# Turning the state's attention weights with 32x32 blocks and on-chip transfers, in batches 2 to 7

## The chip, the cores and the metric

The kernel runs on one core of one Trainium2 chip. The metric is the device time of one execution in microseconds (us); lower is better. All data is float32. The core has five engines that work side by side and meet at semaphores: TensorE (PE in the profile, with its weight loads as PEld), VectorE (DVE), ScalarE (ACT), GpSimd (POOL) and SyncE (SP), which here only issues transfers.

## The reference

Two things are computed one after the other. First a small attention between 512 tokens and 32 states, in 8 batches of 8 heads with 64 dimensions. It is read in both directions: the tokens read the states (`xread`), and the states read the tokens (`sread`). Then every row of the joined result goes through a gated feed-forward layer with 2048 hidden columns.

```python
# x: (8, 8, 512, 64), state: (8, 8, 32, 64)
scores = scale * np.matmul(x, state.transpose(0, 1, 3, 2))
a = softmax(scores)
xread = np.matmul(a, state)
scores2 = scale * np.matmul(state, x.transpose(0, 1, 3, 2))
a2 = softmax(scores2)
sread = np.matmul(a2, x)
attn_out = np.concatenate([xread, sread], axis=2)
...
x = attn_out.transpose(0, 2, 1, 3).reshape(8 * 544, 512)
h = x @ w_in          # 512 x 2048
g = h * np.cos(h)
out = g @ w_out       # 2048 x 512
```

(`softmax` stands for the lines that subtract the maximum, take the exponential and divide by the sum.) The change is about one step on the way to `sread`: for `a2 @ x` on TensorE, the weights `a2` must lie with the tokens on the partitions, and they come out of the exponential with the states on the partitions.

## The kernel before, in words

**Tiles and steps.** Rows of tokens are worked on in 8 batches (`b`), and the hidden columns in 16 tiles of 128. So there are 16 steps per batch, numbered 0 to 15 here, and 16 more for the states' own rows at the end. In every step TensorE computes one hidden tile (`hidden`, L462), ScalarE and VectorE turn it into `h * cos(h)` (`gate`, L468; `gate2`, L471; `gate3`, L476 and L477; `gate4`, L483), and TensorE multiplies tiles of three steps earlier with blocks of `w_out` (`product`, L527). The hidden tile lies in one of two PSUM banks, so the hidden matmul of step s needs that `gate4` of step s-2 is done. The second layer uses a recursive block scheme over pairs of batches (an even and an odd one): in odd batches there are extra differences of gated tiles (`minus`, L489), some on VectorE and some on GpSimd, and finished sums are turned and stored (`store`, L554 and L560), four transfers for one turned tile.

**Attention beside it.** The attention of batch b+1 is computed during the steps of batch b, spread over the steps by a plan that is written out by hand: `plan(b)` returns for every step what TensorE (`pe`), ScalarE (`x_act`, `y_act`) and VectorE (`x_dve`, `y_dve`) do besides. Within a step the program order is: hidden matmul, `pe`, `gate`, `gate2`, `x_act`, `x_dve`, `gate3`, one pending store, `gate4`, differences, `y_act`, `y_dve`, then products. Each engine keeps that order. "Batch b" below always means the steps of batch b, in which the attention of batch b+1 is worked on.

**The parts that matter.** Buffers: `xT` (128 partitions, 4 x 512) holds first the transposed tokens of a batch; later its first half is `spread` and then `a2T`, its second half `z2`. `z2` has heads and states on the partitions (32 states for each of 4 values of k, and j = 0 or 1 in the columns) and the 512 tokens in the columns. `a2T` has the 128 tokens of a group c on the partitions.

- `load_tokens` (L284): 16 transfers into `xT`, followed by `load_x` (L112), 4 transfers. Both are issued on SyncE right after `reads` 1 of the batch before, in `part` (L449 to L453). `tokens_turned` (L293) then turns `xT` in 32x32 blocks on VectorE.
- `scores` (L311), `max1`, `spread1` (L331), `shift`, `max2`, `exps` (L352, L357), `sums` (L325, L367), a second `spread1`, and `norm1` (L375), which reads `spread`, the first half of `xT`.
- `turn` (L381): eight 128x128 transposes of `z2` on TensorE into the two PSUM banks `at`; `turn_kept` (L386): two copies of ScalarE from there into `a2T`.
- `reads` (L398): two times 8 matmuls of `a2T` with the tokens `x_b`, into `at`; `keep` (L409) takes the result away on VectorE; `keep2` and `keep3` (L415, L420) turn it into `sT`.
- `products` (L311) multiply state and `w_in` for the first layer, and also use the `at` banks: in batches from 2 on at steps 0, 4, 9 and 14.

Before the change, batches 2 to 6 run the parts `tokens_turned` at steps 1 and 2 (batch 1: at 2 and 3), `scores` at 5, the second `spread1` at 8 in `y_dve`, `norm1` at 9 in `x_dve`, `turn` at 10, `reads` 0 at 11, `reads` 1 and `keep` at 12, and `keep2` at 15. Batch 1 follows the same steps from 5 on. Batch 0 has its own plan, for its own attention's end and that of batch 1.

SyncE works through one queue in program order: stores, `load_tokens`, `load_x`; the loads of the weights are over after the first steps of batch 1, but for two near the end.

Of the kernel before, what the change touches and what calls it, by code (L numbers as in the profile page):

```python
# [23 lines left out]
def kernel(  # L24
# [8 lines left out]
    nc = tc.nc  # L33

    B, H, S, D = x.shape
    Ns = state.shape[2]
    Dm, Dff = moe_w_in.shape
    P = 128
    NK = Dm // P
# [206 lines left out]
    class Attention:  # L246
# [141 lines left out]

        def reads(self, j):
            cols = slice(2 * D * j, 2 * D * j + 2 * D)
            for c in range(NC):
                x_c = self.x_b[:, c].rearrange("p (k j) d -> p j k d", j=2)
                for k in range(0, NK, 2):
                    rows = slice(Ns * k, Ns * k + 2 * Ns)
                    nc.tensor.matmul(  # L398
                        out=at[0][rows, cols], lhsT=self.a2T[:, j, c, rows],
                        rhs=x_c[:, j, k:k + 2], start=(c == 0),  # L400
                        stop=(c == NC - 1), tile_position=(0, Ns * k))
# [324 lines left out]
    def plan(b):  # L726
        pe, x_act, y_act, x_dve, y_dve = [
            {s: [] for s in range(NF)} for _ in range(5)]

        def prod(s, b, nt, *bank):  # L730
            pe[s].append((b, "products", nt) + bank)
            if b == 1 and nt > 0:
                x_dve[s].append((b, "products_taken", nt) + bank)
            else:
                x_act[s].append((b, "products_kept", nt) + bank)

        def pairs(s, b, name, kept, i):
            pe[s] += [(b, name, i), (b, name, i + 1)]
            x_act[s].append((b, kept, i))
            y_act[s].append((b, kept, i + 1))  # L740

        def early(b, s):
            if b == 1:
                pairs(s[0], b, "tokens", "tokens_kept", 0)
                pairs(s[1], b, "tokens", "tokens_kept", 2)
            else:
                for k in range(NK):
                    to = (x_dve, y_dve)[k % 2]
                    to[s[k // 2]].append((b, "tokens_turned", k))
            pe[s[2]].append((b, "scores"))  # L750
            x_dve[s[2]].append((b, "max1"))
            x_dve[s[3]].append((b, "spread1"))
            y_dve[s[3]].append((b, "shift"))
            x_dve[s[4]].append((b, "max2"))
            y_act[s[4]].append((b, "exps"))
            x_dve[s[5]].append((b, "sums"))
            y_dve[s[5]].append((b, "spread1"))
            x_dve[s[6]].append((b, "norm1"))

        def late(b, s):  # L760
            pairs(s[0], b, "turn", "turn_kept", 0)
            pe[s[1]].append((b, "reads", 0))
            pe[s[2]].append((b, "reads", 1))
            x_dve[s[2]].append((b, "keep"))
            if len(s) > 3:
                turned(b, s[3])

        def turned(b, s):
            pe[s].append((b, "keep2"))
            x_act[s].append((b, "keep3"))  # L770


        if b == 0:
            pe[0].append((0, "products", 0, SIDE, HC, WC))
            y_dve[0].append((0, "products_taken", 0, SIDE, HC, WC))
            prod(7, 0, 2, SIDE)
            prod(11, 0, 3)
            prod(13, 1, 0, MAIN)
            late(0, (1, 2, 3, 4))
            early(1, (5, 6, 7, 8, 9, 10, 11))  # L780
            late(1, (12, 13, 14))
        else:
            bank = (SIDE,) if b == 1 else ()
            if b == 1:
                turned(1, 0)
            prod(0, b, 1, *[MAIN for _ in bank])
            prod(4, b, 2, *bank)
            prod(9, b, 3, *bank)
            if b + 1 < B:
                prod(14, b + 1, 0)  # L790
                early(b + 1, (1 + (b == 1), 2 + (b == 1), 5, 6, 7, 8, 9))
                late(b + 1, (10, 11, 12, 15))
        return pe, x_act, y_act, x_dve, y_dve


# [20 lines left out]
    for step, t in enumerate(all_tiles):  # L816
        s = step % NF
        if s == 0 and t.b < B:
            steps = plan(t.b)
# [81 lines left out]
```

## Time and profile before

| | |
|---|---|
| median of 3 runs | 798.88 us (798.44 to 799.73) |
| the profiled execution's own time | 797.16 us |
| its span, first to last instruction | 795.4 us |
| mean granted TensorE clock | 0.992 |
| L381, transposes of `z2` on TensorE | 64, 273 ns each as listed, 8.3 us |
| L386, copies of the turned weights on ScalarE | 16, 573 ns each, 9.2 us |
| L398, `reads` on TensorE | 256, 279 ns each as listed, 17.5 us |
| L293, turning of the tokens on VectorE, 128x512 | 24, 703 ns each |
| L331, `spread1` on VectorE, 128x1024 | 16, 1237 ns each |
| L284, token transfers of 64 KB | 96, median 2.3 us from issue to landing |
| L560, stores of 64 KB | 128, median 2.0 us from issue to landing |

How to read the profile: the page gives each engine's busy time and share of the span, then the chain of work that ended last, followed back from the end to what released each instruction. Groups of instructions are listed by line, with mean duration and the idle time ahead of them. A timeline row gives start, length, engine, line, operation, tiles, shapes and how many instructions of that kind follow one another; a bracket at its end names the idle time before it and what ended it. A matmul of float32 data appears as two instructions, a transpose as one, so one hidden tile is a row of `x4` and the turning of one batch a row of `x8`. Matmuls are pipelined: the length of a row goes beyond the start of the next.

### The profile page before, as it was taken

Reading aid. Unit: us, or ns where it says so; the run is one execution under the profiler, and the core shown is the slowest. Engines: PE = TensorE matmul, PEld = TensorE weight load, DVE = VectorE, ACT = ScalarE, POOL = GpSimd, SP = SyncE. Lnnn points to the kernel's source line nnn. Section 1 sums busy time; section 2 is a strip of 40 time slices with the busy share of each in tenths; the row PEclk is TensorE's granted clock in tenths of the full one; section 3 lists DMA queues with packets and bytes.
Section 4 is the critical chain, followed back from the end, with each engine's and each line's share of the span. In section 5 each row is a group of like instructions: output and inputs, shape, how many; then the busy total and the mean of one; then the engine's idle time right before and its main releaser. Section 6 shows DMA issues by size and latency. Waiting matters only on the chain.

```text
span 795.4 us, 7553 instructions
## 1 busy us (share of the span) xinstructions
PE 767.1 (96%) x2654; PEld 339.8 (43%) x2654; DVE 437.5 (55%) x689; ACT 389.5 (49%) x626; POOL 178.3 (22%) x119
## 2 busy tenths in 40 slices
PE   8879889999999999999999999999999999999996
PEld 4333333343444444444344434444444444455553
DVE  5779886742554466743564467735554446432431
ACT  3877954644455444734463436443563445322222
POOL 3243357775000000451000000650000004610200
PEclk9999999999999999999999999999999999999999
DMA  8485371032010611150002410340100114000021
GB/s 237 159 227 196 110 155 28 0 55 53 0 26 5 116 24 16 30 103 0 14 13 48 85 27 3 54 78 0 27 0 1 27 27 131 1 0 15 13 47 33
DMA packets 161957, 43.49 MB, mean 55 GB/s; under 512 B 153920, under 2 KB 153920, under 8 KB 161920
## 3 DMA queue, kind: packets, MB, share of 16 engines
q1 hardware_dynamic: 161216, 42.75, 24.7%
q8 instruction: 21, 0.34, 0.2%
q10 hardware_dynamic: 576, 0.13, 0.1%
q0 software_dynamic: 128, 0.13, 0.1%
q14 instruction: 16, 0.13, 0.1%
HBM read 34.08 MB, written 8.91 MB: 54 GB/s over the span
## 4 chain that ended last, share of the span: by engine, by line
PE 79%; DVE 10%; ACT 7%; issue 1%; DMA 1%; POOL 0%; SPq 0%; DVEq 0%; POOLq 0%
PE o L527 44%; PE h L462 26%; PE at L311 4%; PE o L644 3%; DVE q L471 2%; PE at L398 2%; DVE g_all L483 1%; ACT q L476 1%; DVE xT L331 1%; ACT q L477 1%; DVE aT L375 1%; ACT q L468 1%; ACT L477 1%; DVE w_in L234 1%; ACT xT L357 1%
## 5 line engine op out<-in xcount | busy, mean ns | idle before, releaser
L462 PE MATMUL h<-aT,sw 128*128 128x512 f32 x512 | 245.8, 603 | 14.9 <-DVE g_all L483 12.3
L527 PE MATMUL o<-g_all,w_out 128*128 128x512 f32 x512 | 236.4, 598 | 1.2 <-POOL w_out L239 1.2
L468 ACT ACTIVATE q<-h 128x512 f32<-128x512 f32 (+1 forms) x144 | 82.2, 571 | 268.2 <-PE h L462 268.2
L489 POOL TENSOR_TENSOR g_all<-g_all 128x512 f32<-128x512 f32 x80 | 112.1, 1421 | 452.4 <-DVE g_all L483 448.8
L471 DVE SCALAR_TENSOR_TENSOR q<-q,h 128x512 f32<-128x512 f32 (+1 forms) x144 | 94.2, 654 | 206.0 <-ACT q L468 205.8
L527 PE MATMUL o<-g_all,s 128*128 128x512 f32 x384 | 177.3, 598 | 0.0
L483 DVE TENSOR_TENSOR g_all<-h,q 128x512 f32<-128x512 f32 (+1 forms) x144 | 94.8, 658 | 122.3 <-ACT q L477 116.3
L462 PEld LDWEIGHTS h<-aT,sw 128*128 128x128 f32 x512 | 97.1, 192 | 141.6 <-issue 110.1
L527 PEld LDWEIGHTS o<-g_all,w_out 128*128 128x128 f32 x512 | 94.0, 190 | 126.6 <-issue 119.0
L476 ACT ACTIVATE q<-q 128x512 f32<-128x512 f32 (+1 forms) x144 | 87.5, 608 | 97.2 <-DVE q L471 97.2
L527 PEld LDWEIGHTS o<-g_all,s 128*128 128x128 f32 x384 | 70.8, 190 | 91.7 <-issue 87.5
L477 ACT ACTIVATE q<-q,halfpi 128x512 f32<-128x512 f32 (+1 forms) x144 | 100.5, 698 | 4.5
L239 POOL TENSOR_TENSOR w_out<-w_out,s 128x1024 int32<-128x1024 int32 x10 | 23.9, 2389 | 82.3 <-DVE w_out L234 79.6
L489 DVE TENSOR_TENSOR g_all<-g_all 128x512 f32<-128x512 f32 x48 | 33.2, 692 | 1.6
L436 ACT COPY sw<-at 128x512 f32<-128x512 f32 x50 | 26.8, 588 | 9.0 <-PE at L311 9.0
L462 PE MATMUL h<-sT,w_in 128*128 128x256 f32 x128 | 30.2, 379 | 0.0
L644 PE MATMUL o<-w_out,g_all 128*128 128x512 f32 x64 | 29.6, 592 | 0.0
L462 PEld LDWEIGHTS h<-sT,w_in 128*128 128x128 f32 x128 | 24.3, 190 | 10.1 <-issue 6.2
L311 PE MATMUL at<-w_in,stT 64*32 64x512 f32 x400 | 27.9, 616 | 0.0
L239 POOL TENSOR_TENSOR w_in<-w_in,s 128x1024 int32<-128x1024 int32 (+1 forms) x10 | 19.4, 1936 | 32.1 <-DVE w_in L234 22.1
L533 DVE SCALAR_TENSOR_TENSOR held<-o,held 128x512 f32<-128x512 f32 x40 | 25.3, 676 | 2.3 <-PE o L527 2.3
L554 DVE STREAM_TRANSPOSE ot<-held 128x512 f32<-128x512 f32 x32 | 22.2, 693 | 0.0
(85 smaller groups left out, 444.5 us busy)
## 6 DMA issues: line engine op xcount, KB each, us to landing
out_dram<-ot SPq DMA_DIRECT2D x136, 64.0 KB, 2.0
g_all<-in_moe_w_out_dram SPq DMA_DIRECT2D x8, 1024.0 KB, 5.0
g_all<-in_moe_w_in_dram SPq DMA_DIRECT2D x6, 1024.0 KB, 5.3
xT<-in_x_dram SPq DMA_DIRECT2D x96, 64.0 KB, 2.3
x_b<-in_x_dram SPq DMA_DIRECT2D x24, 256.0 KB, 4.5
x_b<-in_x_dram SPq DMA_DIRECT2D x16, 128.0 KB, 3.9
g_all<-in_moe_w_in_dram SPq DMA_DIRECT2D x4, 512.0 KB, 6.0
x_b<-in_moe_w_out_dram SPq DMA_DIRECT2D x1, 1024.0 KB, 5.7
```

Source lines behind the costliest of these rows:

```text
L239: nc.gpsimd.tensor_tensor(bits, bits, e.bitcast(I32), op=ALU.add)
L311: nc.tensor.matmul(out=(to or at)[j][Ns * k:Ns * k + Ns, 0:n], lhsT=w[D * j:D * j + D, self.b, Ns * k:Ns * k + Ns], rhs=r(slice(D * j, D * ...
L436: (copy or nc.scalar.copy)(sw_of[self.b, nt][:, j, c0:c1], to[j][:, 0:c1 - c0])
L462: nc.tensor.matmul(out=t.hp, lhsT=t.lhs(i), rhs=t.rhs(i), start=(i == 0), stop=(i == t.kn - 1))
L468: nc.scalar.activation(t.q, t.hp, func=ACTF.Copy, bias=MAGIC)
L471: nc.vector.scalar_tensor_tensor(out=t.q, in0=t.q, scalar=MAGIC, in1=t.hp, op0=ALU.subtract, op1=ALU.subtract)
L476: nc.scalar.activation(t.q, t.q, func=ACTF.Abs)
L477: nc.scalar.activation(t.q, t.q, func=ACTF.Sin, bias=halfpi, scale=-TWO_PI)
L483: nc.vector.tensor_tensor(t.g, t.hp, t.q, op=ALU.mult)
L489: engine.tensor_tensor(out, a, b, op=ALU.subtract)
L527: nc.tensor.matmul(out=acc[bank][ch], lhsT=w[:, i, P * ch:P * ch + P], rhs=g.g, start=(i == 0), stop=(i == NH - 1))
L644: nc.tensor.matmul(out=acc[MAIN][i], lhsT=t.g[:, P * i:P * i + P], rhs=w_out[:, :, t.f, :], start=(n == 0), stop=(n == NF - 1))
```

## The change

For batches 2 to 7 `turn` and `turn_kept` are no longer put into the plan. In their place VectorE turns `z2` within itself in 32x32 blocks (`turn_blocks`), after the second `spread1`, and 16 transfers on SyncE (`turn_moved`) bring the blocks from `z2` to their partitions in `a2T`, after `norm1`. Each transfer takes the 32 partitions of one k and the blocks of one q (a group of 32 partitions of the target), for both j and all four c: 32 partitions with 8 runs of 32 elements on either side, 32 KB. `reads`, `keep` and what hangs on them go one step later, `tokens_turned` from steps 1 and 2 to steps 2 and 3 in batches 2 to 6. `keep2` stays at 15. Batches 0 and 1 are turned as before.

```diff
@@ class Attention
+        def turn_blocks(self):
+            blocks = self.z2.rearrange("p j (t i) -> p (j t) i", i=32)
+            nc.vector.transpose(out=blocks, in_=blocks)
+
+        def turn_moved(self):
+            nq = P // 32
+            src = self.z2.rearrange("p j (c q n) -> p q (j c) n", q=nq, n=32)
+            dst = self.a2T.rearrange("p j c m -> p (j c) m")
+            for k in range(NK):
+                rows = slice(Ns * k, Ns * k + Ns)
+                for q in range(nq):
+                    nc.sync.dma_start(out=dst[32 * q:32 * q + 32, :, rows],
+                                      in_=src[rows, q])
@@ def early(b, s)
             x_dve[s[5]].append((b, "sums"))
             y_dve[s[5]].append((b, "spread1"))
             x_dve[s[6]].append((b, "norm1"))
+            if b > 1:
+                y_dve[s[5]].append((b, "turn_blocks"))
+                x_dve[s[6]].append((b, "turn_moved"))
 
         def late(b, s):
-            pairs(s[0], b, "turn", "turn_kept", 0)
+            if b < 2:
+                pairs(s[0], b, "turn", "turn_kept", 0)
@@ def plan(b)
                 prod(14, b + 1, 0)
-                early(b + 1, (1 + (b == 1), 2 + (b == 1), 5, 6, 7, 8, 9))
-                late(b + 1, (10, 11, 12, 15))
+                early(b + 1, (2, 3, 5, 6, 7, 8, 9))
+                late(b + 1, (11, 12, 13, 15))
```

## The prediction, made before the result was known

> **What bounds the kernel now.** I read the page first (engine shares, the chain of waits by line), then the groups with shapes kept apart, then the timeline of the steps that the change touches, once in an even batch and once in an odd one.
>
> ```profile
> PE 767.1 (96%) x2654; PEld 339.8 (43%) x2654; DVE 437.5 (55%) x689; ACT 389.5 (49%) x626; POOL 178.3 (22%) x119
> ...
> PE 79%; DVE 10%; ACT 7%; issue 1%; DMA 1%; POOL 0%; SPq 0%; DVEq 0%; POOLq 0%
> ```
>
> TensorE holds the end: 79% of the chain. VectorE holds 10%, so there are places where it releases TensorE, and the steps in question must be looked at one by one. First the even batch 4, steps 10 and 11 (rows are start, length, engine and line):
>
> ```profile
> 413.10 0.65 DVE L471 SCALAR_TENSOR_TENSOR q<-q,h 128x512 f32<-128x512 f32 x1
> 413.68 1.21 DVE L375 TENSOR_TENSOR aT<-aT,xT 128x1024 f32<-128x1024 f32 x1
> 413.92 1.88 PE L462 MATMUL h<-aT,sw 128*128 128x512 f32 x4
> 415.64 1.04 PE L381 MATMUL at<-ident,xT 128*128 128x128 f32 x8
> 416.51 3.60 PE L527 MATMUL o<-g_all,w_out 128*128 128x512 f32 x8
> 419.95 1.88 PE L462 MATMUL h<-aT,sw 128*128 128x512 f32 x4
> ```
>
> Starts on TensorE follow one another without a gap. The eight transposes of L381 hold it from 415.64 to 416.51, 0.87 us, though each is listed with 273 ns: they overlap. The same steps in the odd batch 3:
>
> ```profile
> 326.02 3.01 POOL L489 TENSOR_TENSOR g_all<-g_all 128x512 f32<-128x512 f32 x2 [132.10 <-DVE g_all L483]
> ...
> 326.58 1.24 DVE L331 STREAM_TRANSPOSE xT<-m 128x1024 f32<-128x1024 f32 x1
> 327.74 0.65 DVE L471 SCALAR_TENSOR_TENSOR q<-q,h 128x512 f32<-128x512 f32 x1
> 327.90 1.04 PE L381 MATMUL at<-ident,xT 128*128 128x128 f32 x8
> 328.31 1.80 DVE L375 TENSOR_TENSOR aT<-aT,xT 128x1024 f32<-128x1024 f32 x1
> ...
> 330.66 0.65 DVE L483 TENSOR_TENSOR g_all<-h,q 128x512 f32<-128x512 f32 x1
> ...
> 331.36 1.98 PE L462 MATMUL h<-aT,sw 128*128 128x512 f32 x4 [0.70 <-DVE g_all L483]
> ```
>
> Here VectorE runs back to back and TensorE waits for its gate product L483, transposes included. Batch 5 repeats this (wait 0.71 at 502.43), batch 1 too (0.98 at 160.30). Last, SyncE, which will issue the new transfers:
>
> ```profile
> L284 SPq DMA_DIRECT2D xT<-in_x_dram x96: 311/487/1432, 98.0 to 519.2; - x96
> ...
> DMA to landing us min/median/max: 1.9/2.3/4.9
> ...
> 8.71 0.44 SPq L127 DMA_DIRECT2D s<-in_state_dram  x1
> ```
>
> An issue costs about 0.49 us of SyncE for 512 runs of 128 bytes, and still 0.44 for the 32 KB state loads.
>
> **What the Trainium skill says.** "TensorE: Matmul & The Clock Gate", Part 4, gives about 275 ns for a transpose inside a kernel; the row has 273, but eight take 0.87 and not 2.2 us. "Trainium Kernel Development and Optimization", Performance Expectations, explains the gap: matmul busy time is a bad measure because matmuls are pipelined. So I count starts. "SBUF — State Buffer", section "SBUF: two separate sides", says that a VectorE operation with two SBUF inputs and a GpSimd operation that reads SBUF exclude each other: this trace agrees, since L375 takes 1.80 us and 2.11 us (batch 1) beside L489 on GpSimd, against 1.21 without. "DMA: Bandwidth & Descriptors", "Issuing engines are not separate DMA queues", calls the sequencer's time to initiate a DMA usually small; here 16 issues make 7 us, and they are what I count.
>
> **The change part by part.** The sum is made against the profiled execution, 797.16 us (span 795.4). The runs' median, 798.88, is 1.72 above it; I add the difference to the median.
>
> *Removed, PE and ACT.* Eight transposes in six batches. In the steps that feed batches 3, 5 and 7 (run in 2, 4, 6) TensorE has no gap, so 3 x 0.87 = -2.6 us. In batches 1, 3, 5 the following h matmul waits for L483 anyway: 0. The two copies of L386 (0.57 us each) leave ScalarE, which these waits don't name: 0; were ScalarE next in the chain it would be at most 1.1 us per batch below.
>
> *Added, turn_blocks.* The trace of before has no transposition of z2; the nearest row is L331, of the same 128x1024, with 1.24 us and 1.16 from its start to the next operation's (326.58 to 327.74). Bounds: 1.16 and 1.4 (twice the 0.70 of L293). I take 1.16. It stands right after spread1, and behind it on VectorE are gate2 of step 9 (L471), norm1 (L375) and gate4 of step 9 (L483), which frees the h bank for step 11. Even batches: L483 would end at about 417.2 instead of 415.96, and h of step 11, now at 419.07, doesn't see it: 0. If that cover went, 1.2 each. Odd batches: L471 moves to 328.90 and L375 to 329.47. GpSimd is done by 329.03, so L375 takes 1.21 and ends at 330.68 instead of 330.11: +0.57 in batches 3 and 5. In batch 1, GpSimd runs to 158.56 and L375 ends at 159.90 instead of 159.64: +0.26. Sum +1.4 us.
>
> *Added, 16 transfers.* They overwrite `spread`, so the first waits for norm1; the wait is at the head of SyncE's queue with a store of four DMAs behind it (due after step 9 in odd batches), and no later store comes before step 15, so nobody feels that. Each has 256 runs of 128 bytes, 32 KB. Issue time: the first of a burst 0.36 (L284's fast ones with the gap), then between 0.36 and 0.53 (487 ns and a gap of 0.04). State loads of 128 runs take 0.44 + 0.04, 512 runs 0.53: I take 0.49. Landing: 1.8 (fastest store) to 2.3 (L284) from the start of the issue; I take 2.0. So 0.36 + 14 x 0.49 + 2.0 = 9.2 us from norm1's end to the last landing. The second matmul of reads 0 needs every transfer, as each carries both j and all c.
>
> Reads 0 are now at step 12. Even: h(11) 419.07, o 420.79, h(12) 424.22, reads at 426.0. norm1 ends at 416.05, transfers land at 425.3: hidden, with 0.7 to spare. Odd, batch 3: h(11) 331.93, o 333.76, h(12) 337.2, reads at 339.0; transfers leave at 330.72 and land at 339.9: TensorE stands 0.9 us; batch 5 the same. Batch 1: reads at 167.6, landed at 169.1: 1.5. Sum +3.3. More semaphores than before stand ahead of these reads; an event wait of L398 is 51 ns, so between 0 and 0.4 us a batch, mostly beside the h matmul: +0.3 in all.
>
> *Moved.* reads, keep and, through reads 1, the 16 load_tokens and 4 load_x issues go one step later, tokens_turned too, except after batch 1. From the end of reads 1 these take 16 x 0.53 + 4 x 0.8 + 2.3 = 14 us, and five steps of some 5 us lie before tokens_turned; scores at step 5 still have two steps. 0. keep now has one step until the products of step 14 need its bank: reads 1 ends near 433.6 on the even timeline, keep costs 0.16 + 0.17 + 1.19 and is done near 435.8, the bank is wanted at 437: 0, with about 1 us of cover.
>
> Sum: -2.6 + 1.4 + 3.3 + 0.3 = +2.4, so 799.6 for a profiled execution and 801.3 us for the median.
>
> **Rivals.**
>
> *A, the forecast:* gain in even batches, chain and late transfers in odd ones. Landing and pitch at their ends move each odd stall by 0.8 us, and can open the same in even ones: 799.3 to 805.
>
> *B, the transfers are in time everywhere.* Pitch 0.36 or less: the last lands after 0.36 + 14 x 0.36 + 2.0 = 7.4, before the reads of batch 3 by 0.9. Left are -2.6 + 1.4: 797.7. For it: isolated issues take 311 ns. Against: in bursts of four or more they never did.
>
> *C, the other side: turn_blocks is hidden too.* If the odd chain has room that I don't see (ScalarE freed of copies, gates running ahead), all six batches gain 0.87: -5.2, 793.7. It decides where the gate product of step 9 ends before TensorE wants the bank, 2.3 us earlier in batch 3 than I expect. Against: three waits on L483 in the trace.
>
> *D, transfers at a slower pitch,* 0.62 us (a copy from SBUF to SBUF costs more, or waits for an earlier one that shares rows): 0.36 + 14 x 0.62 + 2.3 = 11.3. Stalls of 1.4 in even batches, 3.1, 3.1 and 3.6 in odd: 4.2 + 9.8 - 1.2 = +12.8, 811.7. The trace of before shows no transfer inside SBUF, so it can't be excluded.
>
> That the change doesn't do what it says would show as 64 transposes of L381 instead of 16; the diff leaves no way for it.
>
> **How the numbers follow.** A 0.53, B 0.18, C 0.11, D 0.18. About what a measurement can tell from no change is 0.2%, 1.6 us. Slower by more: D, and A but for 0.05: 0.66. Within: B, and that 0.05: 0.22. Faster: C and the edge of B: 0.12. Predicted is A, 801.3. The range from 797 to 810 leaves out C and the upper part of D, 0.2 together; A's own is 799.3 to 805.
>
> **What would show it.** Right: L381 only in batches 0 and 1; a STREAM_TRANSPOSE of 128x1024 on xT with 1.24 us; L375 at 1.21 in odd batches; waits of h on L483 longer by 1 us and more there; a wait of L398 on the new DMAs in batches 1, 3 and 5 and none in 2, 4, 6. Wrong: an issue pitch far from 0.49, waits in even batches, or no wait of L398 at all.

## The result, and the profile after

| | before | after |
|---|---|---|
| median of 5 runs | 798.88 us (797.0 to 799.73) | 817.9 us (816.92 to 820.25) |
| ratio, 95% interval | | 1.025 [1.0229, 1.0271] |
| span of the profiled execution | 795.4 us | 816.1 us |
| mean granted TensorE clock | 0.992 | 0.984 |

The kernel became slower by 19 us, where 2.4 had been expected. (One of the 14 executions of experiment 3 below took 2037 us, in a slow state, and is not in its ratio; all others are fast, but for the single one of experiment 4, whose state is unknown.)

First the page of the changed kernel, its engine shares and its chain of waits (lines after the change: L478 is the hidden matmul, L543 the products, L414 `reads`, L393 `turn_blocks`, L402 the 16 transfers, L499 `gate4`):

```profile
PE 769.8 (94%) x2606; PEld 337.7 (41%) x2606; DVE 440.9 (54%) x695; ACT 383.1 (47%) x614; POOL 178.2 (22%) x119
...
PE 66%; ACT 11%; DVE 10%; SPq 7%; issue 3%; DMA 2%; POOL 0%; ACTq 0%; DVEq 0%
```

TensorE has 48 instructions fewer and a *longer* listed busy time, a first sign that something runs slower as well as later. SyncE, 0% of the chain before, now holds 7%. The one line that waits for it, and SyncE's own durations (first the waits: total, times, longest; then the line's instructions, ns as min/median/max):

```profile
PE at L414 <- DMA xT<-xT: 13.4, 6, 4.1
```

```profile
L402 SPq DMA_DIRECT2D xT<-xT x96: 585/609/1744, 161.0 to 616.7; - x96
...
DMA to landing us min/median/max: 1.9/2.0/3.7
```

Six waits for six turned batches: the transfers are late every time. One issue takes 0.609 us, and almost none takes less. The timeline of batch 4, an even one:

```profile
424.39 1.20 DVE L393 STREAM_TRANSPOSE xT<-xT 128x1024 f32<-128x1024 f32 x1
426.09 1.21 DVE L375 TENSOR_TENSOR aT<-aT,xT 128x1024 f32<-128x1024 f32 x1
427.44 10.43 SPq L402 DMA_DIRECT2D xT<-xT  x16
...
437.32 0.43 PE L414 MATMUL at<-x_b,xT 128*64 128x128 f32 x2
439.51 1.06 PE L414 MATMUL at<-x_b,xT 128*64 128x128 f32 x14 [1.76 <-DMA xT<-xT]
440.50 3.70 PE L543 MATMUL o<-g_all,w_out 128*128 128x512 f32 x8
```

`norm1` ends at 427.30; 16 issues then occupy SyncE for 10.43 us (0.65 from one to the next), and the last one's data lands 1.9 us after its issue began. TensorE has done the first two matmuls of `reads` 0 and stands. (The row lists 1.76 us of idle time, counted from modelled ends; by the starts of its instructions TensorE loses 2.16 us.) In the odd batch 3 the same wait comes on top of a longer chain on VectorE:

```profile
334.63 1.20 DVE L393 STREAM_TRANSPOSE xT<-xT 128x1024 f32<-128x1024 f32 x1
...
336.33 1.21 DVE L375 TENSOR_TENSOR aT<-aT,xT 128x1024 f32<-128x1024 f32 x1
...
338.08 0.65 DVE L499 TENSOR_TENSOR g_all<-h,q 128x512 f32<-128x512 f32 x1
...
338.79 2.96 PE L478 MATMUL h<-aT,sw 128*128 128x512 f32 x4 [2.12 <-DVE g_all L499]
341.54 4.37 PE L543 MATMUL o<-g_all,s 128*128 128x512 f32 x8
```

Look at the lengths: four hidden matmuls take 2.96 us, in the even batch 1.88. The windows right behind the wait say why (start and end, length, busy time of PE, PEld, DVE, ACT and POOL, granted clock, DMA share, GB/s):

```profile
338.00:340.00 2.00, 1.21 (x3) 0.66 (x4) 1.97 (x4) 0.31 (x1) 1.19 (x1) 0.92 0.21 33
340.00:342.00 2.00, 2.00 (x4) 0.85 (x3) 0.55 (x2) 1.88 (x4) 1.82 (x2) 0.50 0.32 49
342.00:344.00 2.00, 2.00 (x4) 0.72 (x3) 1.97 (x4) 0.45 (x1) 1.72 (x1) 0.73 0.31 49
```

After TensorE had stood for 2.12 us its clock fell to half for some 3.4 us. In batch 5 a single issue took 1.74 us, `reads` waited 4.12 us and the clock fell behind that wait:

```profile
527.65 1.94 PE L414 MATMUL at<-x_b,xT 128*64 128x128 f32 x14 [4.12 <-DMA xT<-xT]
```

The starts of the hidden matmuls of both traces, laid side by side, give the account (after minus before, us):

| where | batch 1 | batch 3 | batch 5 | even, each of 3 |
|---|---|---|---|---|
| transposes of TensorE gone | 0 | 0 | 0 | -0.88 |
| `turn_blocks` in the chain to the hidden matmul of step 11 | +0.22 | +0.54 | +0.54 | 0 |
| TensorE slower after that wait | +1.70 | +1.69 | 0 | 0 |
| step 12 waiting for VectorE to take a sum (held, L556) out of its bank | 0 | 0 | +0.5 | 0 |
| `reads` 0 waiting for transfers, with a clock fall in batch 5 | +2.65 | +2.17 | +6.02 | +2.16 |
| sum | +4.57 | +4.40 | +7.06 | +1.28 |

With 1.0 in the first batch, which differs by that much from one execution to the next, it is 1.0 + 4.57 + 4.40 + 7.06 + 3 x 1.28 = 20.9, against 20.7 between the spans.

The rows of this table add up by place; they don't say what each would save alone. In all six batches `reads` 0 goes on 0.1 to 0.35 us after the last landing (in batch 3 at 349.75 after 349.40), and the landing follows from `norm1` and SyncE, not from TensorE. In batches 1 and 3 the slow stretch of TensorE lies ahead of `reads` 0, so it only uses up time in which TensorE would have stood for the transfers: without it the wait in the last row but one would be longer by about as much. Only the clock fall of batch 5, behind the wait, comes on top.

### The profile page after: what moved, and what is told of

The parts are those of the page before. It is cut to its first block, busy times and chain, and to the rows that moved or that the text cites. A ratio compares the mean times of both kernels' runs of the same rounds, so it can differ in the third digit from the quotient of the medians.

```text
span 816.1 us, 7629 instructions
## 1 busy us (share of the span) xinstructions
PE 769.8 (94%) x2606; PEld 337.7 (41%) x2606; DVE 440.9 (54%) x695; ACT 383.1 (47%) x614; POOL 178.2 (22%) x119
## 4 chain that ended last, share of the span: by engine, by line
PE 66%; ACT 11%; DVE 10%; SPq 7%; issue 3%; DMA 2%; POOL 0%; ACTq 0%; DVEq 0%
PE o L543 36%; PE h L478 21%; SPq L402 7%; PE o L660 3%; PE at L311 3%; DVE q L487 2%; ACT q L492 2%; ACT q L493 2%; PE at L414 2%; DVE xT L331 1%; DMA xT<-xT 1%; ACT q L484 1%; ACT L493 1%; ACT xT L357 1%; DVE g_all L499 1%
## 5 line engine op out<-in xcount | busy, mean ns | idle before, releaser
L478 PE MATMUL h<-aT,sw 128*128 128x512 f32 x512 | 248.2, 608 | 18.8 <-DVE g_all L499 16.2
L543 PE MATMUL o<-g_all,w_out 128*128 128x512 f32 x512 | 236.4, 598 | 0.1
L543 PE MATMUL o<-g_all,s 128*128 128x512 f32 x384 | 179.5, 603 | 0.2 <-DVE held L556 0.2
L499 DVE TENSOR_TENSOR g_all<-h,q 128x512 f32<-128x512 f32 (+1 forms) x144 | 94.8, 658 | 123.8 <-ACT q L493 120.3
L478 PEld LDWEIGHTS h<-aT,sw 128*128 128x128 f32 x512 | 97.5, 193 | 146.6 <-issue 111.4
L543 PEld LDWEIGHTS o<-g_all,w_out 128*128 128x128 f32 x512 | 94.2, 190 | 127.2 <-issue 123.9
L543 PEld LDWEIGHTS o<-g_all,s 128*128 128x128 f32 x384 | 72.2, 193 | 96.1 <-issue 90.5
L414 PE MATMUL at<-x_b,xT 128*64 128x128 f32 x256 | 20.8, 288 | 13.4 <-DMA xT<-xT 13.4
L478 PE MATMUL h<-sT,w_in 128*128 128x256 f32 x128 | 30.2, 379 | 0.0
L478 PEld LDWEIGHTS h<-sT,w_in 128*128 128x128 f32 x128 | 24.3, 190 | 10.1 <-issue 6.2
L414 PEld LDWEIGHTS at<-x_b,xT 128*64 128x64 f32 x256 | 15.5, 141 | 26.9 <-issue 20.6
```

The costliest lines, as they stand in the source:

```text
L414: nc.tensor.matmul(out=at[0][rows, cols], lhsT=self.a2T[:, j, c, rows], rhs=x_c[:, j, k:k + 2], start=(c == 0), stop=(c == NC - 1), tile_p ...
L478: nc.tensor.matmul(out=t.hp, lhsT=t.lhs(i), rhs=t.rhs(i), start=(i == 0), stop=(i == t.kn - 1))
L499: nc.vector.tensor_tensor(t.g, t.hp, t.q, op=ALU.mult)
L543: nc.tensor.matmul(out=acc[bank][ch], lhsT=w[:, i, P * ch:P * ch + P], rhs=g.g, start=(i == 0), stop=(i == NH - 1))
```

## The experiments

Ratios are to the kernel before, run beside them on the same chip (its median: 798.12 us beside experiments 1 to 4, 798.52 beside 5 to 8). The ratios differ by up to 0.15% from the quotients of the medians.

**1. Only the new step numbers.** In the kernel before:

```diff
-                early(b + 1, (1 + (b == 1), 2 + (b == 1), 5, 6, 7, 8, 9))
-                late(b + 1, (10, 11, 12, 15))
+                early(b + 1, (2, 3, 5, 6, 7, 8, 9))
+                late(b + 1, (11, 12, 13, 15))
```

> The kernel before with only the new step numbers: tokens_turned at 2 and 3, turn on TensorE at 11, reads at 12 and 13 and keep at 13. Theory L (the 16 transfers land late): the steps alone cost nothing, 798 to 800 us, ratio 0.998 to 1.002. Rival S (the move of reads, keep and the token loads by one step costs): most of the 19 us shows here, above 808 us. Rival V (VectorE's turn_blocks and what it holds up): as theory L.

Measured: 801.08, ratio 1.0035 [1.0023, 1.0046], more than theory L's 798 to 800 and far below rival S's 808. The even batches don't move. Each odd one loses 0.87 us, because the eight transposes at step 11 no longer lie under the wait ahead of that step's hidden matmul. The loads, `tokens_turned` and `keep` that also moved cost nothing. The 0.87 isn't part of the 19 us, since the changed kernel has no such transposes; so the moves explain none of them.

**2. Only the block transposition.** `turn_blocks` added to the kernel before, with the turn on TensorE left in (the state's rows of batches 2 to 7 then differ from the reference):

```diff
             x_dve[s[6]].append((b, "norm1"))
+            if b > 1:
+                y_dve[s[5]].append((b, "turn_blocks"))
```

> The kernel before with turn_blocks added on VectorE and nothing else; TensorE still turns z2, which is block-turned by then, so the sread of batches 2 to 7 is another one. Theory L: VectorE's chain in batches 1, 3 and 5 grows by 0.2 to 0.55 us each, together +1.3, about 800 us; TensorE's wait there is 1.2 to 1.3 us and no 2.1, since its transposes fill the rest, so its clock should hold (with a fall of the clock 1.7 us more in each batch that has it, up to 805). Rival V: more than half of the 19 us, above 808. Rival S: 799.

Measured: 799.49, ratio 1.0022 [1.001, 1.0034]; +0.22, +0.54 and +0.54 at step 11 of the odd batches, 0 in the even ones. Batch 1, timeline:

```profile
160.87 1.98 PE L466 MATMUL h<-aT,sw 128*128 128x512 f32 x4 [0.62 <-DVE g_all L487]
```

The chain's part of the prediction (+0.26, +0.57, +0.57) holds to 0.04 us each. And the matmuls take their usual 1.98: with transposes in the gap TensorE stands 0.62 us (1.2 to 1.3 had been expected) instead of 2.1, and its clock stays at 1.00.

**3. The changed kernel with `reads` 0 a step later,** so that both halves run at step 13:

```diff
-                late(b + 1, (11, 12, 13, 15))
+                late(b + 1, (11, 13, 13, 15))
```

> The changed kernel with reads 0 put at step 13 beside reads 1, some 5 us later, so that the 16 transfers have landed. Theory L: the waits of reads on the transfers (2.2 us in each of five batches, 4.5 in batch 5) go; left are -0.87 in batches 2, 4 and 6, +1.3 of VectorE's chain and 1.7 us for each fall of TensorE's clock after the 2.1 us gaps of batches 1, 3 and 5: 798 to 804 us. Rivals V and S: it stays above 812, since VectorE's work and the later steps are still there.

Measured: 797.05, ratio 0.9996 [0.9985, 1.0007], 20.9 below the changed kernel, from one number, and just under the 798 to 804 expected. No wait of `reads` on a transfer is left. The even batches gain 1.22 each: the 0.88 of the transposes, and 0.34 that I put down to the two halves standing together (no run shows it alone). Batches 3 and 5 keep +0.68 each, batch 1 +1.4 to 1.6. Batch 1, timeline and window:

```profile
161.27 3.47 PE L478 MATMUL h<-aT,sw 128*128 128x512 f32 x4 [2.08 <-DVE g_all L499]
```

```profile
160.00:164.00 4.00, 2.73 (x4) 1.28 (x5) 2.55 (x5) 2.02 (x4) 2.64 (x3) 0.70 0.16 25
```

Here the clock falls behind 2.08 us of standing; in batch 3 of the same run the gap is 2.12 and no fall follows, though in the changed kernel one did. The traces tell the two apart. The three falls of the changed kernel start at 162.17, 339.67 and 527.40, which is 52 and 55 times 3.413 us from one to the next, and each lasts 3.41 us; the other traces fit such a grid too. Cut into its windows, the two gaps of experiment 3 look like this (batch 1, then batch 3):

```profile
158.21:161.62 3.41, 1.33 (x4) 0.45 (x3) 3.41 (x6) 1.83 (x3) 1.35 (x2) 1.00 0.00 0
161.62:165.03 3.41, 3.41 (x5) 1.33 (x4) 1.48 (x3) 2.09 (x4) 3.41 (x3) 0.50 0.29 45
```

```profile
328.88:332.29 3.41, 2.00 (x5) 0.57 (x3) 3.41 (x5) 1.61 (x3) 1.24 (x2) 1.00 0.04 6
332.29:335.70 3.41, 2.70 (x7) 1.27 (x8) 1.94 (x4) 1.59 (x4) 2.68 (x2) 1.00 0.25 39
```

The gap of batch 1 (159.19 to 161.27) lies in one window and leaves TensorE 1.33 us of listed busy time there; that of batch 3 (330.88 to 333.00) is split between two. In the ten traces kept here (one execution each), from step 1 of batch 1 to the end of batch 7, all nine falls follow a window with 1.34 us or less, and no window with 1.55 us or more is followed by one. There are twelve gaps of 2.1 us ahead of step 11: five lie inside one window and cost 1.7 us more, seven are split by a boundary and cost nothing more. Where the grid lies differs from trace to trace, so which of the two happens is chance.

**4. What makes the issue dear.** Forms of the 16 transfers by batch of attention; batch 3 takes the same runs of 128 bytes from HBM, batch 4 stays inside SBUF with one run of 1 KB in each partition, batch 5 has runs of 1 KB from HBM, and 2, 6 and 7 keep the change's own. The altered ones bring other data into the weights, so the state's rows of batches 3 to 5 aren't the reference's.

```diff
-                    nc.sync.dma_start(out=dst[32 * q:32 * q + 32, :, rows],
-                                      in_=src[rows, q])
+                    to, get = dst[32 * q:32 * q + 32, :, rows], src[rows, q]
+                    if self.b == 3:
+                        get = x[0, 2 * k, 0:256, 0:32].rearrange(
+                            "(g t) d -> t g d", t=32)
+                    if self.b in (4, 5):
+                        to = self.a2T.rearrange("p j c m -> p (j c m)")
+                        to = to[32 * q:32 * q + 32, 256 * k:256 * k + 256]
+                    if self.b == 4:
+                        get = self.z2.rearrange("p j s -> p (j s)")
+                        get = get[rows, 256 * q:256 * q + 256]
+                    if self.b == 5:
+                        get = x[0, 2 * k].rearrange("(p t) d -> p (t d)", t=4)
+                        get = get[32 * q:32 * q + 32]
+                    nc.sync.dma_start(out=to, in_=get)
```

> The changed kernel; the 16 transfers of batches 3, 4 and 5 take another form, so their sread is another one: batch 2, 6, 7 as in the change (SBUF to SBUF, 32 partitions x 8 runs of 128 bytes); batch 3 the same runs but read from x in HBM; batch 4 SBUF to SBUF with one run of 1 KB per partition; batch 5 from HBM with one run of 1 KB. All carry 32 KB. Theory R (the issue is paid by the number of runs): batch 3 stays near 0.61 us per issue, batches 4 and 5 fall below 0.45. Theory B (both ends in SBUF cost): batches 3 and 5 fall to 0.45 or so, batch 4 stays near 0.6. Neither: all the same 0.6.

Measured (one run, 810.59), the issue of each form in ns as min/median/max:

```profile
L415 SPq DMA_DIRECT2D xT<-in_x_dram x16: 323/449/878, 250.6 to 258.3; - x16
...
L415 SPq DMA_DIRECT2D xT<-xT x16: 524/588/590, 335.7 to 345.2; - x16
...
L415 SPq DMA_DIRECT2D xT<-in_x_dram x16: 336/419/420, 422.0 to 428.9; - x16
```

From top to bottom: HBM with short runs 449, SBUF with long runs 588, HBM with long runs 419; the change's own form, SBUF with short runs, has 609. The source decides: inside SBUF an issue costs 0.16 to 0.17 us more, while eight times longer runs save 0.02 to 0.03. The waits of `reads` follow: batch 3's transfers (issued in 8.15 us) cost 0.25 in the even batch before it, batch 5's (issued in 7.29, all landed by 430.76, `reads` 0 at 432.0) nothing at all, and that even batch gets its full 0.88. Batch 4's form cost `reads` 0 no wait either, but that says nothing of the price: with 1 KB runs the first eight transfers hold all that `reads` 0 needs, and they had landed (341.96, `reads` 0 at 344.4), while the last landed at 347.03.

**5. Half of the issues on GpSimd.**

```diff
+                queue = nc.sync if k < 2 else nc.gpsimd
                 for q in range(nq):
-                    nc.sync.dma_start(out=dst[32 * q:32 * q + 32, :, rows],
-                                      in_=src[rows, q])
+                    queue.dma_start(out=dst[32 * q:32 * q + 32, :, rows],
+                                    in_=src[rows, q])
```

> The changed kernel with the eight transfers of k = 2 and 3 issued by GpSimd instead of SyncE. Theory L: SyncE's half is issued in 8 x 0.65 = 5.2 us and lands 6.5 us after norm1; GpSimd's half takes 8 issues of 0.56 us or more (its state loads), so 6.5 to 9 us with the landing. Reads 0 come 9.9 us after norm1 in even batches and 8.3 in odd ones, so most of the 2.2 us waits go: 800 to 808 us. If the transfers themselves, and no queue, took the time, nothing changes: 817.

Measured: 811.1, ratio 1.0144 [1.0128, 1.0159], above the 800 to 808 expected. The part about lateness was right: the waits of `reads` are gone and the even batches gain their full 0.88. But batches 3 and 5 lose 6.8 and 6.9, and batch 1 loses 1.7, by a clock fall. Batch 3, timeline (the rows of the three engines in order of time):

```profile
333.20 4.64 POOL L403 DMA_DIRECT2D xT<-xT  x8 [2.29 <-ACT q L494]
...
337.23 4.88 DVE L506 TENSOR_TENSOR g_all<-g_all 128x512 f32<-128x512 f32 x1
337.86 3.70 POOL L506 TENSOR_TENSOR g_all<-g_all 128x512 f32<-128x512 f32 x3
...
342.04 0.68 DVE L557 TENSOR_SCALAR held<-o 128x512 f32<-128x512 f32 x1
...
342.77 1.22 PE L544 MATMUL o<-g_all,s 128*128 128x512 f32 x1 [4.43 <-DVE held L557]
```

GpSimd's queue is ordered too. It stands until `norm1` is done (332.53), then issues for 4.64 us, and its differences of gated tiles come in a bunch at 337.86. VectorE's own difference, usually 0.69 us, is listed with 4.88 and ends 0.5 us after GpSimd's; behind it is the held sum L557 whose bank TensorE wants; behind that wait of 4.43 us its clock falls as well. "SBUF — State Buffer", section "SBUF: two separate sides", of the Trainium skill states that such operations of the two engines exclude each other; these rows fit that, though the excluded VectorE operation is listed with the earlier start; no run here took the two apart.

**6. The clock by itself.** Experiment 3 with eight transposes whose result nobody reads, put at step 10 of the odd batches, where TensorE stands anyway:

```diff
         def late(b, s):
...
+            if b > 1 and b % 2 == 0:
+                pe[10] += [(b, "turn", 0), (b, "turn", 1)]
```

> The kernel with both reads at step 13, plus eight transposes on TensorE at step 10 of batches 1, 3 and 5 whose results nobody uses (their ScalarE copies are left out). Theory C (TensorE's clock falls in odd batches because without its transposes the wait for the gate product grows to 2.1 us): the filler lies inside that wait and costs nothing, the wait falls to about 1.2 us, no slice has a clock below 0.95 around it, and batch 1 loses its 1.3 us: 796 to 797.5 us. Without C: 0.9 us more for each odd batch, 799.5, or the clock falls all the same.

Measured: 796.08, ratio 0.9965 [0.9952, 0.9977]. Batch 1 went from +1.4 to -0.18. Same timeline row and window as in experiment 3:

```profile
161.58 1.98 PE L478 MATMUL h<-aT,sw 128*128 128x512 f32 x4 [0.62 <-DVE g_all L499]
```

```profile
160.00:164.00 4.00, 3.38 (x9) 1.35 (x8) 2.55 (x4) 2.32 (x6) 2.33 (x2) 1.00 0.14 21
```

More work on the engine that bounds the kernel, and a shorter time: the gap is 0.62 instead of 2.08, the clock 1.00 instead of 0.70, the four matmuls take 1.98 instead of 3.47. Nor was it luck with the grid. In this trace its window is

```profile
158.65:162.06 3.41, 2.79 (x11) 1.30 (x10) 3.41 (x5) 1.82 (x3) 1.37 (x2) 1.00 0.00 0
```

and a gap of 2.08 us that ends at 161.58 would lie inside it too and leave 1.33 us of busy time, the figure behind which experiment 3 has its fall. Batches 3 and 5, where no fall was, stay at +0.69.

**7. `norm1` out of the odd chain, without the change.** In the kernel before, the second `spread1` writes into `z2` (free by then) at the end of step 10:

```diff
+        def spread2(self):
+            self.spread = self.z2
+            self.spread1()
...
-            y_dve[s[5]].append((b, "spread1"))
-            x_dve[s[6]].append((b, "norm1"))
+            if b < 2:
+                y_dve[s[5]].append((b, "spread1"))
+                x_dve[s[6]].append((b, "norm1"))
+            else:
+                y_dve[10] += [(b, "spread2"), (b, "norm1")]
```

> The kernel before, with TensorE's transposes, but for batches 2 to 7 the second spread1 and norm1 are taken out of steps 8 and 9 and put at the end of step 10, with the spread in z2's place. Theory V2 (VectorE's chain at steps 8 and 9 is what holds TensorE in batches 1, 3 and 5): those waits go, 0.7 us in batches 3 and 5 and 1 to 2.8 in batch 1: 794 to 797 us, ratio 0.994 to 0.998. If the waits only move to step 11 or 12: 1.000.

Measured: 798.91, ratio 1.000 [0.9988, 1.0011]. Step 11 of batches 3 and 5 starts 0.86 earlier, step 12 then waits 1.5 for a held sum on VectorE and they end 0.8 later; batch 1 gains 1.2. In these two the wait only moved, and over all nothing was won.

**8. The transfers out of the chain.** The transfers need `z2` turned and `spread` free, not `norm1` as such. So `turn_blocks` and the transfers come at the end of step 8, the second `spread1` goes into the place of `z2` (`spread2` of experiment 7) and `norm1` after it, both at the end of step 12:

```diff
+            if b < 2:
+                y_dve[s[5]].append((b, "spread1"))
+                x_dve[s[6]].append((b, "norm1"))
+            else:
+                y_dve[s[5]] += [(b, "turn_blocks"), (b, "turn_moved")]
+                y_dve[12] += [(b, "spread2"), (b, "norm1")]
...
-                late(b + 1, (11, 12, 13, 15))
+                late(b + 1, (11, 13, 13, 15))
```

> The change put elsewhere: the transfers leave right after turn_blocks at the end of step 8, the second spread1 and norm1 come at the end of step 12 in z2's place, both reads at step 13. Theory L with V2: no wait on transfers (11.7 us from step 8 to landing, step 13 is 20 us later), 0.87 us and the saved change of tile shape in each of six batches (1.2 us in the even batches of the run with both reads at 13), and the odd batches' waits on VectorE gone: 787 to 792 us, ratio about 0.99. If VectorE's 2.4 us at step 12 hold the gates there: 0.995 or more.

Measured: **792.03, ratio 0.9906 [0.9893, 0.9919]**: faster than both kernels, at the upper end of the 787 to 792 expected. Even batches gain 1.22, batches 3 and 5 0.63, batch 1 2.04. Batch 3, timeline:

```profile
327.93 10.43 SPq L406 DMA_DIRECT2D xT<-xT  x16
...
330.56 1.98 PE L482 MATMUL h<-aT,sw 128*128 128x512 f32 x4 [0.80 <-DVE g_all L503]
```

The transfers take their 10.43 us as before, but they start 1.8 us after the hidden matmul of step 10 (326.16) and not 4.6 (337.68 after 333.08 in the changed kernel). The last one lands at 339.65; `reads` begin at 343.27. The wait ahead of step 11 is 0.80 instead of 2.12, and no clock fall comes from step 1 of batch 1 to the end of batch 7.

## Why the prediction was wrong

The direction was right, and so was the mechanism in the odd batches: late transfers at `reads` 0. That the even batches would wait too was not foreseen, and the size was off by 16.6 us at the medians (817.9 against 801.3). By the steps of the prediction:

- *Removed transposes, 3 x 0.87.* Right: 0.88 appears wherever the wait for transfers is gone (experiments 4 and 5). In the changed kernel it is there too, under 2.16 us of a new wait.
- *`turn_blocks`, +1.4.* Right: +1.3, shown alone by experiment 2. It takes 1.20, L375 1.21 in the odd batches, as said. Beside GpSimd's differences it had taken 1.80 and 2.11.
- *Landing 2.0.* Right, 1.92; until `reads` 0 goes on, 0.1 to 0.35 us more pass.
- *Issue pitch 0.49: the failing step.* "State loads of 128 runs take 0.44 + 0.04, 512 runs 0.53: I take 0.49." It was read off transfers that come from HBM and applied to a copy inside SBUF. Experiment 4 shows that 0.49 (0.449 + 0.04) is just what these 16 transfers cost when they come from HBM; inside SBUF they cost 0.65. The first isn't cheaper either (0.59 to 0.74 where 0.36 was taken). So the last landing comes 11.9 us after `norm1` (427.30 to 439.2 in batch 4), not 9.2. Put into the prediction's own sum, these 2.7 us turn the "0.7 to spare" of the even batches into waits of 2.0, and the 0.9, 0.9 and 1.5 of the odd ones into 3.6, 3.6 and 4.2: -2.6 + 1.4 + 17.4 + 0.3 = +16.5, an estimate of 815.4 us. Measured are 2.16 in each even batch, and 3.86 and 4.35 in batches 3 and 1 (the third to fifth rows of the table together). By this estimate 14.1 us of the miss of 16.6 are this one term.
- *What lies beyond it.* In batch 5 one issue took 1.1 us more than the others, and behind the wait of 4.1 us the clock fell: 6.5 in the same rows instead of 3.6. The sum had no term for the clock. In batches 1 and 3 the falls were drawn by waits of 2.1 us, and the later wait for the transfers covered them, so the absent term isn't what made the prediction miss; where no transfer is waited for, it shows (experiments 3 and 6). The Trainium skill, "TensorE: Matmul & The Clock Gate", Part 1, names idle windows of about 3.4 us on a free-running counter as the cause of half clock. The traces agree with half (0.50) and with a grid of 3.41 us; but the windows that did it here needn't be idle: 1.34 us of listed busy time in one was still too little.
- *Semaphores, +0.3, and the moved steps, 0.* The moves cost nothing (experiment 1); no separate cost of semaphores can be seen.

Rival D had the mechanism and the pitch, 0.62, to 0.03 us, at a chance of 0.18; its 811.7 falls short by the even waits (2.16 instead of 1.4 each), by some 0.8 us in each odd wait, and by the slow issue and the clock fall of batch 5. A is false in its even batches, B and C are false as well: no transfer was in time, and the odd chain did take `turn_blocks`. What was weighed wrongly is the evidence for A over D: there was no row of a copy inside SBUF in the trace, so the nearest row was of another kind, and its ends were taken as bounds of the price.

Two things stay open. Why an issue inside SBUF is dearer, no run shows; rows shared in the target aren't it, since the short runs from HBM went to the same rows at 0.449. Nor why one issue in batch 5 took 1.74 us, though the traces have a hint: it runs from 521.64, and at 521.39 a transfer of 16 KB of instructions (queue q8 of the profile's list of DMA queues) had begun. The long issues in batch 5 of experiments 3, 4 and 8 (1.05, 1.69 and 1.32 us) start 0.1 to 0.3 us behind such a transfer as well; in experiment 6 it came at 492.68, ahead of the burst, and none of that batch's 16 issues was long. One such transfer at the start of a burst (experiment 8, 243.29) lengthened nothing, and no experiment took the cause apart.

## What to carry to other kernels

Count the issues of a burst of small transfers, not their bytes: 16 x 0.65 us of one queue is 10.4 us, five times the landing, so the burst needs 12 us of lead, more than two steps of this kernel, and should hang on nothing that comes late. A price for a transfer holds for its kind of source; where the trace has no such row, the range has to hold the dearer kind. And a wait of 2.1 us on TensorE can cost nearly twice its length, so look at the granted clock behind each new gap, unless a later wait covers it anyway; a little useless work in the gap can be cheaper than none.

## What the runs showed of the hardware

- Copying inside SBUF takes 0.609 us of SyncE for each issue, from HBM 0.449, at the same size and runs; 1 KB runs in place of 128 bytes bring 0.588 and 0.419. The Trainium skill, "DMA: Bandwidth & Descriptors", "Issuing engines are not separate DMA queues", calls this time usually small beside the transfer; for a burst of 16 here it was the whole matter.
- Issues on GpSimd took 0.584 us, hardly less, and blocked that engine's own work for 4.64 us per eight.
- TensorE's clock fell to 0.50 for 3.41 us behind five of twelve gaps of 2.1 us (batch 1 of the changed kernel and of experiments 3, 4 and 5, and batch 3 of the changed kernel), those that lay inside one window of the 3.41 us grid. All nine falls from step 1 of batch 1 to the end of batch 7 followed a window with at most 1.34 us of listed busy time of TensorE, none a window with 1.55 us or more. Transposes count as such busy time here: eight of them in the gap brought the window from 1.33 to 2.79 us (experiment 6).
